# Attention and gated FFN on one core: the RMS scale by a power on GpSimd, the gain at the transposes, scores issued ahead

## The chip, the core and the metric

One NeuronCore of a Trainium2 chip runs the whole program. The metric is the device time of one execution in microseconds. PE is TensorE (matmuls, and transposes as matmuls against an identity), DVE is VectorE, ACT is ScalarE, POOL is GpSimd, and SP only issues DMAs. Each engine works through its own instructions strictly in the order in which the kernel was written, since the whole program stands under a manual schedule; engines wait for each other by semaphores.

## What is computed

Eight batches of causal attention (8 heads, 576 positions, head size 64) whose scores carry a decay, and on its output, read as 4608 tokens of 512, an RMS norm with a gain and a gated FFN:

```
scores = q @ k.T / 8 + min(-(cum_i - cum_j), 0)      # cum: running sum of max(s, 0)
x   = softmax(scores, causal) @ v                    # per batch and head
xn  = x / sqrt(mean(x * x) + 1e-6) * rms_g
out = (silu(xn @ w_gate) * (xn @ w_val)) @ w_out     # 512 -> 1536 -> 512
```

The kernel writes exp(score) as exp(q.k/8) times a weight of the key, which is folded into v (`vw`), so no row maximum is taken. Checks at the end (`check_decay`, `check_all`) set a flag when the inputs don't allow that; a slow general path follows then. It isn't entered here.

## The kernel before

**Stages.** The FFN works in nine chunks of 512 tokens, attention in eight batches of 576. After a start with batch 0 the program alternates between two kinds of stage:

- F(c), c = 0 to 8: the first FFN products of chunk c (`ffn1`). A group (`ffn1_group`, L294) is the gate and value products of one block of 128 hidden units, then Silu on ACT (L302), then the product with the value half on DVE (L303), which frees one of two PSUM buffers `psD`. Chunks 0 to 3 take 256 tokens a group (24 groups), the later ones 512 (12 groups).
- A(b), b = 1 to 7: the attention of batch b, woven with the second FFN product (`ffn2_steps`, 48 matmuls) of chunk b-1. F(8) and its second product end the program.

**Attention.** Eight units of one pair of heads and one half of the queries each. `unit_scores` issues the score matmuls into `psD`, an Exp on ACT and the causal mask on POOL (`affine_select`, L231, for the second half of the units L235 too). `unit_av` (L253 to L258) multiplies with `vw` into one of two `psAV` buffers, and DVE divides by the row sum and writes `x_blk`. Before, AV of unit u stands ahead of the scores of unit u+2.

**RMS norm.** A batch has five blocks of 128 tokens. After unit 4 blocks 0 and 1 are complete: ACT squares and sums them (L265) and `att_alpha` (L268) computes 1/sqrt on DVE by a bit trick and three Newton steps, twelve instructions on 128x2 numbers, and two that scale `x_blk` (L281). Blocks 2 to 4 follow in the next F stage. `att_out` transposes a scaled block on PE (L288, `psX`) and DVE copies it into `xnT` (L292), the FFN's input. The gain `rms_g` is multiplied into the two weight matrices once, on DVE (`scale_w`, L123).

**What stands beside F(c).** Python lists of functions with a position between 0 and 1 (`fillers`): `ffn1` calls each behind the first group whose share of the stage reaches its position. They are the tail of batch c's norm (`tail_fillers`) and the preparation of batch c+1 (`prep_fillers`): repacking of k and q from runs of six positions to one block per transpose (`prep_pack`, L172, on POOL), transposes with their copies, `prep_v` on POOL, and for the check the largest absolute value of every row of KT and QT (`prep_peak`, L191, on DVE). POOL also issues the loads of k and q (which turn fp32 into bf16), and those of v and the weights at the start.

Of the kernel before, what the change touches and what calls it, by code (L numbers as in the profile page):

```python
# [10 lines left out]
def kernel(  # L11
# [108 lines left out]
    def scale_w(which, lo, hi):  # L120
        dst = (wg_sb, wv_sb)[which]
        for cc in range(CC):
            nc.vector.tensor_scalar(  # L123
                out=dst[:, cc, lo:hi], in0=dst[:, cc, lo:hi],
                scalar1=g_sb[:, cc : cc + 1], scalar2=None, op0=ALU.mult)

    def decay_weights():
# [46 lines left out]

    def prep_transpose(b, which, hp):
        src, dst = ((k_nat, KT), (q_nat, QT))[which]
        pT = ps_t()
        for c in range(KC):
            nc.tensor.matmul(pT[:, c, :], lhsT=src[:, c, 2 * hp : 2 * hp + 2, :].rearrange("p h d -> p (h d)"),  # L179
                             rhs=ident_bf[0:KP, 0:KP], is_transpose=True,  # L180
                             start=(c == 0), stop=(c == KC - 1))
        o = dst[:, hp, 0:S].rearrange("p (t c) -> p t c", c=KC)
        i = pT.rearrange("p c t -> p t c")
# [436 lines left out]
```

## Time and profile before

| what | value |
|---|---|
| median of 2 runs | 527.65 us (526.64 to 528.66) |
| the profiled execution's own time | 528.67 us |
| its span, first to last instruction | 527.0 us |
| PE busy | 401.5 us, 76% |
| DVE busy | 313.6 us, 60% |
| ACT busy | 201.4 us, 38% |
| POOL busy | 164.1 us, 31% |
| mean granted clock of PE | 0.902 |

Busy shares are means over the whole span. PEclk is the share of full speed that PE's clock had in a stretch: 1.00 is 2.4 GHz and 0.50 is 1.2 GHz, the only two levels that the records show; a value between is a mixture in time. A row of a timeline gives start and duration of an instruction (or of some equal ones, x4) in us, and in brackets how long its engine had been idle and what released it.

### The profile page before, as it was taken

The numbers are of one execution on the slowest core, as the hardware profiler recorded it, in microseconds if no ns is written. First come the engines' busy times: TensorE is split into PE (matmuls) and PEld (weight loads), VectorE is DVE, ScalarE is ACT, GpSimd is POOL, SyncE is SP. The second block draws the span as 40 slices with busy tenths as digits, with TensorE's granted clock in tenths as the row PEclk, the third lists the DMA queues.
The fourth block names the chain that finished last, engine by engine and source line by source line (L and its number), as shares of the span: only waits on it lengthen the run. The fifth ranks groups of instructions, "written<-read, shape, count | busy, mean of one in ns | idle before, by whom it ended". The sixth has DMA issues, their size and how long they took to land.

```text
span 527.0 us, 8080 instructions
## 1 busy us (share of the span) xinstructions
PE 401.5 (76%) x3092; PEld 240.3 (46%) x3129; DVE 313.6 (60%) x756; ACT 201.4 (38%) x349; POOL 164.1 (31%) x268
## 2 busy tenths in 40 slices
PE   3556589479965899479956898579947997799895
PEld 2334475248633775258533444235422544343442
DVE  5665886746666584747565484747573666433341
ACT  2532236324562247224552247034722465230220
POOL 8565503830067003820076004900381013000000
PEclk9997999779997799689987799689977998899999
DMA  9999541091014701090006601290100001001002
GB/s 144 195 192 207 110 65 41 21 177 25 1 41 80 142 1 41 21 200 2 21 22 109 112 1 41 38 181 1 41 20 21 1 21 42 20 1 60 22 1 85
DMA packets 53069, 33.77 MB, mean 64 GB/s; under 512 B 29856, under 2 KB 47776, under 8 KB 53024
## 3 DMA queue, kind: packets, MB, share of 16 engines
q0 software_dynamic: 19104, 16.52, 20.2%
q1 hardware_dynamic: 33920, 16.67, 13.0%
q8 instruction: 26, 0.43, 0.3%
q14 instruction: 19, 0.16, 0.1%
HBM read 37.90 MB, written 9.44 MB: 90 GB/s over the span
## 4 chain that ended last, share of the span: by engine, by line
PE 58%; DVE 25%; ACT 7%; issue 5%; POOL 2%; DMA 2%; ACTq 0%; POOLq 0%
PE psD L298 29%; PE psO L322 17%; DVE peak L191 4%; ACT sq_scr L265 4%; DVE x_blk L281 4%; DVE H_sb L303 4%; PE psAV L253 3%; PE psD L224 3%; PE psX L288 3%; DVE al L278 3%; DVE al L276 3%; DVE al L277 2%; ACT E L229 2%; PE psT L179 2%; DMA v_nat<-in_v_dram 2%
## 5 line engine op out<-in xcount | busy, mean ns | idle before, releaser
L302 ACT ACTIVATE S_sb<-psD 128x256 bf16<-128x256 f32 (+1 forms) x156 | 72.2, 465 | 272.3 <-PE psD L298 262.6
L298 PE MATMUL psD<-xnT,wg_sb 128*128 128x256 bf16 (+1 forms) x614 | 129.7, 334 | 13.0 <-DVE H_sb L303 10.7
L303 DVE TENSOR_TENSOR H_sb<-S_sb,psD 128x256 bf16<-128x256 bf16 (+1 forms) x156 | 80.5, 520 | 99.2 <-ACT S_sb L302 98.9
L298 PE MATMUL psD<-xnT,wv_sb 128*128 128x256 bf16 (+1 forms) x620 | 126.7, 330 | 0.2
L231 POOL TENSOR_SCALAR_AFFINE_SELECT E<-E 128x512 bf16<-128x512 bf16 x64 | 40.7, 636 | 262.9 <-ACT E L229 262.8
L322 PE MATMUL psO<-wout_sb,H_sb 128*128 128x512 bf16 x409 | 112.2, 409 | 2.9 <-issue 2.7
L298 PEld LDWEIGHTS <-wg_sb 128*128 128x128 bf16 x624 | 61.8, 104 | 48.2 <-issue 20.1
L298 PEld LDWEIGHTS <-wv_sb 128*128 128x128 bf16 x624 | 64.3, 103 | 38.5 <-issue 4.0
L253 PE MATMUL psAV<-vw,E 128*128 128x65 bf16 x576 | 33.4, 207 | 53.8 <-DVE x_blk L258 48.2
L229 ACT ACTIVATE E<-psD 128x1024 bf16<-128x1024 f32 x64 | 64.4, 1021 | 23.9 <-PE psD L224 23.9
L253 PEld LDWEIGHTS <-E 128*128 128x128 bf16 x576 | 28.1, 106 | 72.8 <-DVE x_blk L258 51.7
L322 PEld LDWEIGHTS <-H_sb 128*128 128x128 bf16 x432 | 39.0, 104 | 46.4 <-issue 14.3
L327 DVE COPY osb<-psO 128x512 f32<-128x512 f32 x36 | 24.8, 689 | 44.5 <-PE psO L322 44.5
L288 PE MATMUL psX<-ident_bf,x_blk 128*128 128x128 bf16 x160 | 20.9, 295 | 35.3 <-DVE x_blk L281 34.7
L197 POOL TENSOR_TENSOR vw<-v_nat,wT 128x512 bf16<-128x512 f32 (+1 forms) x35 | 36.5, 1043 | 3.6 <-DMA v_nat<-in_v_dram 3.5
L288 PEld LDWEIGHTS <-x_blk 128*128 128x128 bf16 x160 | 16.5, 137 | 45.3 <-DVE x_blk L281 38.3
L258 DVE TENSOR_TENSOR x_blk<-psAV,rZ 128x256 bf16<-128x256 f32 (+1 forms) x64 | 31.4, 491 | 2.2
L224 PE MATMUL psD<-QT,KT 64*128 64x256 bf16 (+2 forms) x320 | 26.7, 266 | 1.0 <-DVE H_sb L303 1.0
L265 ACT ACTIVATE sq_scr<-x_blk 128x512 bf16<-128x512 bf16 x40 | 25.0, 626 | 0.8
L185 DVE COPY KT<-psT 128x576 bf16<-128x576 bf16 x32 | 24.0, 749 | 1.6 <-PE psT L179 1.5
L172 POOL COPY q_nat<-q_raw 96x768 bf16<-96x768 bf16 x28 | 23.5, 838 | 1.8 <-DMA q_raw<-in_q_dram 1.8
L257 DVE RECIPROCAL rZ<-psAV 128x4 f32<-128x4 f32 (+1 forms) x64 | 11.7, 183 | 20.7 <-PE psAV L253 20.7
(72 smaller groups left out, 350.2 us busy)
## 6 DMA issues: line engine op xcount, KB each, us to landing
out_dram<-osb SPq DMA_DIRECT2D x36, 256.0 KB, 2.0
v_nat<-in_v_dram SPq DMA_DIRECT2D x24, 256.0 KB, 8.0
k_raw<-in_k_dram POOLq DMA_DIRECT2D x7, 576.0 KB, 6.4
q_raw<-in_q_dram POOLq DMA_DIRECT2D x7, 576.0 KB, 10.0
v_nat<-in_v_dram POOLq DMA_DIRECT2D x8, 256.0 KB, 14.3
wg_sb<-in_moe_w_gate_dram POOLq DMA_DIRECT2D x4, 384.0 KB, 14.0
wv_sb<-in_moe_w_val_dram POOLq DMA_DIRECT2D x4, 384.0 KB, 15.6
wout_sb<-in_moe_w_out_dram POOLq DMA_DIRECT2D x2, 768.0 KB, 19.1
```

Of the source, the lines that this page charges most:

```text
L197: eng.tensor_tensor(out=vw[0:n, sc, :, 0:64], in0=v_nat[0:n, b % 2, sc, :, :], in1=wb.unsqueeze(2).to_broadcast([n, H, D]), op=ALU.mult)
L224: nc.tensor.matmul(st[:, j, c0 : c0 + q1 - q0], lhsT=KT[rs, hp, kb * 128 : kb * 128 + 128], rhs=QT[rs, hp, q0:q1], start=(i == 0), stop=(i ...
L229: nc.scalar.activation(out=E, in_=st, func=AF.Exp, scale=0.125)
L231: nc.gpsimd.affine_select(out=diag, in_=diag, pattern=[[0, 4], [1, 128]], compare_op=ALU.is_ge, fill=0.0, base=0, channel_multiplier=-1)
L253: nc.tensor.matmul(AV[:, j, qb - q0, :], lhsT=E[:, j, c0 : c0 + 128], rhs=vw[:, kb, h, :], start=(j == 0 and i == 0), stop=(j == 1 and i = ...
L258: nc.vector.tensor_tensor(out=a.x[:, q0 : q0 + nq, hp * 128 : (hp + 1) * 128].rearrange("p t (j d) -> p j t d", j=2), in0=AV[:, :, :, 0:64 ...
L265: nc.scalar.activation(out=sq_scr, in_=a.x[:, tb, :], func=AF.Square, accum_out=a.ss[:, tb : tb + 1])
L288: nc.tensor.matmul(X[:, cc, :], lhsT=a.x[:, tb, cc * 128 : (cc + 1) * 128], rhs=ident_bf, is_transpose=True, start=(cc == 0), stop=(cc == ...
L298: nc.tensor.matmul(P[:, j, 0:n], lhsT=w[:, cc, fb * 128 : (fb + 1) * 128], rhs=xnT[:, cc, t0 + o : t0 + o + n], start=(cc == 0), stop=(cc ...
L302: nc.scalar.activation(out=sl[:, 0:n], in_=P[:, 0, 0:n], func=AF.Silu)
L303: nc.vector.tensor_tensor(out=Ht[:, fb, o : o + n], in0=sl[:, 0:n], in1=P[:, 1, 0:n], op=ALU.mult)
L322: nc.tensor.matmul(O, lhsT=Ht[:, fb, tb * 128 : (tb + 1) * 128], rhs=wout_sb[:, fb, :], start=(fb == 0), stop=(fb == FB - 1))
```

## The change

- `att_alpha` is two GpSimd instructions: mean plus epsilon, and that to the power -0.5. The scaling of a block is a function of its own, `att_scale`, on DVE: for blocks 0 and 1 it stands two units later than the squares (behind unit 6), for blocks 2 to 4 right ahead of each block's transpose.
- `rms_g` is multiplied in where `xnT` is written; `scale_w` is gone.
- k and q of batches 2 to 7 are loaded in blocks of 128 positions (ten DMAs a batch, each run 64 numbers long, into double buffers) and need no repacking; batches 0 and 1 are still repacked, on DVE, with the free end of `xnT` as buffers. The loads of batch c+2 stand at 0.1 of F(c).
- The scores of unit u+2 stand ahead of AV of unit u, and the second FFN product is dealt out 8, 4, 6 matmuls around the first scores.
- The check keeps the largest absolute value of QT only, in the A stage; for k it takes sums of squares on ACT (`prep_norm`).
- A group of chunks 0 to 3 holds two hidden blocks, so that Silu and product work on 512 columns; the weights come in two pieces each instead of four.

```diff
     def att_alpha(a, t0, t1):
...
+        nc.gpsimd.tensor_scalar(out=m, in0=a.ss[:, t0:t1], scalar1=1.0 / DM, scalar2=1e-6,
                                 op0=ALU.mult, op1=ALU.add)
-        nc.vector.tensor_scalar(out=y.bitcast(i32), in0=m.bitcast(i32), scalar1=-0.5,
-                                scalar2=1597463007.0, op0=ALU.mult, op1=ALU.add)
...
+        nc.gpsimd.tensor_tensor(out=y, in0=m, in1=mhalf[:, 0 : t1 - t0], op=ALU.pow)
+
+    def att_scale(a, tb):
+        nc.vector.tensor_scalar(out=a.x[:, tb, :], in0=a.x[:, tb, :],
+                                scalar1=a.al[:, 1, tb : tb + 1], scalar2=None, op0=ALU.mult)
...
-        nc.vector.tensor_copy(out=xnT[:, :, c0 : c0 + 128 - p0], in_=X[:, :, p0:128])
+        nc.vector.tensor_tensor(
+            out=xnT[:, :, c0 : c0 + 128 - p0], in0=X[:, :, p0:128],
+            in1=g_sb.unsqueeze(2).to_broadcast([128, CC, 128 - p0]), op=ALU.mult)
...
     def tail_fillers(a, lo, hi):
-        fns = [lambda: [att_square(a, tb) for tb in (2, 3, 4)], lambda: att_alpha(a, 2, 5)]
-        fns += [lambda tb=tb: att_out(a, tb) for tb in (2, 3, 4)]
+        fns = [lambda tb=tb: att_square(a, tb) for tb in (2, 3, 4)]
+        fns += [lambda: att_alpha(a, 2, 5)]
+        fns += [lambda tb=tb: (att_scale(a, tb), att_out(a, tb)) for tb in (2, 3, 4)]
         return spread(fns, lo, hi)
...
         for u in range(2 * HP):
-            unit_av(a, u)
             if u + 2 < 2 * HP:
                 unit_scores(a, u + 2)
+            unit_av(a, u)
             if u == HP:
-                att_square(a, 0)
-                att_square(a, 1)
+                for tb in (0, 1):
+                    att_square(a, tb)
                 att_alpha(a, 0, 2)
+            if u == HP + 2:
+                for tb in (0, 1):
+                    att_scale(a, tb)
...
             if c + 2 < B:
-                fillers.append((0.65 if c else 0.96, lambda b=c + 2: (load_kq(b, 0), load_kq(b, 1),
-                                                       load_v(b, nc.sync))))
+                for w in range(2):
+                    fillers.append((0.1, lambda b=c + 2, w=w: load_kq(b, w)))
+                fillers.append((0.1, lambda b=c + 2: load_v(b, nc.sync)))
```

The order on GpSimd (POOL) behind the attention of batch 0, before: loads of k and q (L98), of `wout` (L111) and of v (L105) for batch 1, and then the repacking.

```order
L235 AFFINE_SELECT E<-E 128x2x64
L98 DMA k_raw<-in_k_dram 96x8x384
L98 DMA q_raw<-in_q_dram 96x8x384
L111 DMA wout_sb<-in_moe_w_out_dram 128x6x512 x2
L105 DMA v_nat<-in_v_dram 128x8x64 x4
L105 DMA v_nat<-in_v_dram 64x8x64
L172 COPY k_nat<-k_raw 96x6x128
```

The same place now; `xnT` stands for the borrowed buffers of k and q, L105 loads k and q of batch 2, L318 and L320 are the scale of blocks 2 to 4 of batch 0.

```order
L111 DMA xnT<-in_k_dram 96x8x384
L111 DMA xnT<-in_q_dram 96x8x384
L124 DMA wout_sb<-in_moe_w_out_dram 128x6x512 x2
L118 DMA v_nat<-in_v_dram 128x8x64 x4
L118 DMA v_nat<-in_v_dram 64x8x64
L105 DMA k_nat<-in_k_dram 128x8x64 x4
L105 DMA k_nat<-in_k_dram 64x8x64
L105 DMA q_nat<-in_q_dram 128x8x64 x4
L105 DMA q_nat<-in_q_dram 64x8x64
L318 TENSOR_SCALAR al<-ss 128x3
L320 TENSOR_TENSOR al<-al,mhalf 128x3
```

Ten more DMA issues stand ahead of the scale on POOL; in F(1) to F(5) the same ten stand ahead of it, without the nine rows of batch 1 and `wout`.

The order on VectorE (DVE) late in A(1), before: the end of the twelve-step scale and the scaling of blocks 0 and 1, and behind them the reciprocals and products (L257, L258) that free the `psAV` buffers.

```order
L277 TENSOR_TENSOR al<-al 128x2
L278 SCALAR_TENSOR_TENSOR al<-al 128x2
L281 TENSOR_SCALAR x_blk<-x_blk,al 128x512 x2
L257 RECIPROCAL rZ<-psAV 128x6
L258 TENSOR_TENSOR x_blk<-psAV,rZ 128x2x3x64
L257 RECIPROCAL rZ<-psAV 128x6
L258 TENSOR_TENSOR x_blk<-psAV,rZ 128x2x3x64
```

The same place now, with L305 and L306 for these two lines, L378 for the copy of a finished output block, and L323 for the scaling.

```order
L305 RECIPROCAL rZ<-psAV 128x6
L306 TENSOR_TENSOR x_blk<-psAV,rZ 128x2x3x64
L378 COPY osb<-psO 128x512
L305 RECIPROCAL rZ<-psAV 128x6
L306 TENSOR_TENSOR x_blk<-psAV,rZ 128x2x3x64
L323 TENSOR_SCALAR x_blk<-x_blk,al 128x512 x2
L305 RECIPROCAL rZ<-psAV 128x6
L306 TENSOR_TENSOR x_blk<-psAV,rZ 128x2x3x64
```

Three of the last units were freed behind the scale; now only the last one is, and behind the scaling alone.

The order on VectorE (DVE) at the start of F(1), before: products of the first two groups, the scale of three blocks, then products and copies into `xnT` in turn.

```order
L278 SCALAR_TENSOR_TENSOR al<-al 128x3
L281 TENSOR_SCALAR x_blk<-x_blk,al 128x512 x3
L303 TENSOR_TENSOR H_sb<-S_sb,psD 128x256
L292 COPY xnT<-psX 128x4x128
L303 TENSOR_TENSOR H_sb<-S_sb,psD 128x256 x2
L292 COPY xnT<-psX 128x4x128
L303 TENSOR_TENSOR H_sb<-S_sb,psD 128x256
L292 COPY xnT<-psX 128x4x64
```

The same place now: L352 is the product of a group, L323 the scaling of one block, L334 the write into `xnT`.

```order
L352 TENSOR_TENSOR H_sb<-S_sb,psD 128x2x256 x3
L323 TENSOR_SCALAR x_blk<-x_blk,al 128x512
L334 TENSOR_TENSOR xnT<-psX,g_sb 128x4x128
L352 TENSOR_TENSOR H_sb<-S_sb,psD 128x2x256
L323 TENSOR_SCALAR x_blk<-x_blk,al 128x512
L334 TENSOR_TENSOR xnT<-psX,g_sb 128x4x128
L352 TENSOR_TENSOR H_sb<-S_sb,psD 128x2x256
L323 TENSOR_SCALAR x_blk<-x_blk,al 128x512
L334 TENSOR_TENSOR xnT<-psX,g_sb 128x4x64
```

The three scalings stood together, ahead of a product; now each stands behind the product of the group just issued.

## Rows read from the trace of the kernel before

**Rows 1.** Seven A stages by windows: stretch, its length, busy time per engine, PEclk, DMA, GB/s.

```profile
81.40:107.33 25.93, 18.08 (x166) 9.67 (x169) 16.71 (x39) 12.25 (x15) 17.31 (x29) 0.87 0.09 32
...
427.29:448.97 21.68, 17.69 (x166) 9.70 (x169) 12.91 (x39) 12.46 (x15) 6.07 (x12) 0.92 0.10 37
sum 180.57, PE 128.57 PEld 68.78 DVE 109.85 ACT 86.41 POOL 112.83; mean PE 18.37 PEld 9.83 DVE 15.69 ACT 12.34 POOL 16.12
```

**Rows 2.** Seven F stages, F(1) to F(7), by windows.

```profile
165.78:198.51 32.73, 27.52 (x253) 22.83 (x252) 20.94 (x54) 12.83 (x33) 2.70 (x5) 0.90 0.49 82
...
sum 213.88, PE 182.98 PEld 117.12 DVE 128.72 ACT 79.17 POOL 9.24; mean PE 26.14 PEld 16.73 DVE 18.39 ACT 11.31 POOL 1.32
```

**Rows 3.** F(8), which has nothing beside it, by windows.

```profile
489.44:510.18 20.74, 20.64 (x97) 9.41 (x98) 7.70 (x12) 6.57 (x11) 0.00 (x0) 1.00 0.00 1
```

**Rows 4.** Waits of PE's attention and transposes on VectorE: total us, times, longest.

```profile
PE psAV L253 <- DVE x_blk L258: 48.2, 7, 7.5
...
PE psX L288 <- DVE x_blk L281: 34.7, 9, 4.6
```

**Rows 5.** Timeline of A(2): start, duration, engine, line, operation; in brackets idle time and releaser.

```profile
153.53 0.16 DVE L276 TENSOR_TENSOR al<-al 128x2 f32<-128x2 f32 x1
...
154.90 0.82 POOL L172 COPY k_nat<-k_raw 96x768 bf16<-96x768 bf16 x1
...
155.77 0.73 DVE L276 TENSOR_TENSOR al<-al 128x2 f32<-128x2 f32 x1
...
158.08 2.47 DVE L281 TENSOR_SCALAR x_blk<-x_blk,al 128x512 bf16<-128x512 bf16 x2
...
161.29 0.84 PE L253 MATMUL psAV<-vw,E 128*128 128x65 bf16 x12 [7.48 <-DVE x_blk L258]
```

**Rows 6.** Timeline of A(7).

```profile
440.22 1.00 ACT L229 ACTIVATE E<-psD 128x1024 bf16<-128x1024 f32 x1
...
441.29 0.64 POOL L231 TENSOR_SCALAR_AFFINE_SELECT E<-E 128x512 bf16<-128x512 bf16 x1 [1.39 <-ACT E L229]
...
444.36 0.84 PE L253 MATMUL psAV<-vw,E 128*128 128x65 bf16 x12 [3.33 <-DVE x_blk L258]
```

**Rows 7.** Timeline of F(5), its first groups.

```profile
343.64 0.60 ACT L302 ACTIVATE S_sb<-psD 128x512 bf16<-128x512 f32 x1 [13.93 <-PE psD L298]
...
344.27 0.69 DVE L303 TENSOR_TENSOR H_sb<-S_sb,psD 128x512 bf16<-128x512 bf16 x1 [1.67 <-ACT S_sb L302]
...
348.56 0.88 DVE L281 TENSOR_SCALAR x_blk<-x_blk,al 128x512 bf16<-128x512 bf16 x3
348.97 0.61 PE L288 MATMUL psX<-ident_bf,x_blk 128*128 128x128 bf16 x4 [3.65 <-DVE x_blk L281]
```

**Rows 8.** The stretch behind F(2)'s first wait, by windows.

```profile
170.87:177.70 6.83, 5.12 (x29) 3.88 (x30) 3.67 (x15) 0.77 (x2) 0.00 (x0) 0.50 1.25 233
```

**Rows 9.** Groups by line and form: busy us, mean ns of one, idle before.

```profile
L197 POOL TENSOR_TENSOR vw<-v_nat,wT 128x512 bf16<-128x512 f32 x28 | 29.2, 1042 | 3.6 <-DMA v_nat<-in_v_dram 3.5
...
L292 DVE COPY xnT<-psX 128x512 bf16<-128x512 bf16 x32 | 13.4, 421 | 5.0 <-PE psX L288 5.0
...
L200 POOL COPY vw<-wT 128x8 bf16<-128x8 bf16 x28 | 6.1, 218 | 0.0
```

**Rows 10.** Timeline of GpSimd from 34 to 56 us.

```profile
34.73 1.81 POOL L105 DMA_DIRECT2D v_nat<-in_v_dram  x2
...
39.41 0.88 POOL L105 DMA_DIRECT2D v_nat<-in_v_dram  x1 [1.30 <-DMA wv_sb<-in_moe_w_val_dram]
43.56 0.70 POOL L105 DMA_DIRECT2D v_nat<-in_v_dram  x1 [3.27 <-DMA k_raw<-in_k_dram]
...
55.88 1.04 POOL L197 TENSOR_TENSOR vw<-v_nat,wT 128x512 bf16<-128x512 f32 x1 [3.52 <-DMA v_nat<-in_v_dram]
```

**Rows 11.** The page's table of DMA issues: KB of each, median us from issue to landing.

```profile
v_nat<-in_v_dram SPq DMA_DIRECT2D x24, 256.0 KB, 8.0
...
v_nat<-in_v_dram POOLq DMA_DIRECT2D x8, 256.0 KB, 14.3
```

More of the change, by code (lines that the diff above doesn't have):

```diff
@@ L45 @@
     CUM_MAX = 150.0
-    DOT_MAX = 12.0
+    QK_MAX = 200.0
     pers = ctx.enter_context(tc.tile_pool(name="pers", bufs=1))
@@ L93, in ps_t, with load_kq, load_runs @@
     def ps_t():
-        return pp.tile([128, KC, KP], bf16, name="psT", tag="AT", bufs=2)
-    def load_kq(b, which, h0=0, h1=H):
+        return pp.tile([128, NB * 128], bf16, name="psT", tag="AT", bufs=2)
+    def load_kq(b, which):
+        dst, src = ((k_nat, k), (q_nat, q))[which]
+        for sc in range(NB):
+            n = 128 if sc < 4 else 64
+            nc.gpsimd.dma_start(
+                out=dst[0:n, b % 2, sc, :, :],
+                in_=src[b, :, sc * 128 : sc * 128 + n, :].rearrange("h p d -> p h d"))
+    def load_runs(b, which, h0=0, h1=H):
         dst, src = ((k_raw, k), (q_raw, q))[which]
@@ L118, in load_w, with decay_a @@
                 in_=src[:, lo:hi].rearrange("(cc p) f -> p cc f", p=128))
[L120 to L127, printed above, removed]
+    def decay_a():
         nc.vector.tensor_scalar(out=s_all, in0=s_all, scalar1=0.0, scalar2=None, op0=ALU.max)
@@ L175, in prep_transpose @@
     def prep_transpose(b, which, hp):
-        src, dst = ((k_nat, KT), (q_nat, QT))[which]
+        dst = (KT, QT)[which]
         pT = ps_t()
[L178 to L183, printed above, removed]
+        if b < 2:
+            src = (k_pk, q_pk)[which]
+            t = pT[:, 0:S].rearrange("p (c t) -> p c t", c=KC)
+            for c in range(KC):
+                nc.tensor.matmul(t[:, c, :],
+                                 lhsT=src[:, c, 2 * hp : 2 * hp + 2, :].rearrange("p h d -> p (h d)"),
+                                 rhs=ident_bf[0:KP, 0:KP], is_transpose=True,
+                                 start=(c == 0), stop=(c == KC - 1))
+            o = dst[:, hp, 0:S].rearrange("p (t c) -> p t c", c=KC)
+            i = t.rearrange("p c t -> p t c")
+        else:
+            src = (k_nat, q_nat)[which]
+            for sc in range(NB):
+                n = 128 if sc < 4 else 64
+                nc.tensor.matmul(
+                    pT[:, sc * 128 : sc * 128 + n],
+                    lhsT=src[0:n, b % 2, sc, 2 * hp : 2 * hp + 2, :].rearrange("p h d -> p (h d)"),
+                    rhs=ident_bf[0:n, 0:n], is_transpose=True,
+                    start=(sc == 0), stop=(sc == NB - 1))
+            o, i = dst[:, hp, 0:S], pT[:, 0:S]
@@ L306, in ffn1 @@
     def ffn1(c, plan, fillers):
         Ht = mp.tile([128, FB, DM], bf16, name="H_sb", tag="H_sb", bufs=2)
-        done, total = 0, len(fillers)
-        for i, (o, n, fb) in enumerate(plan):
-            ffn1_group(Ht, c * DM, o, n, fb)
-            while done < total and fillers[done][0] <= (i + 1) / len(plan):
+        fillers = sorted(fillers, key=lambda f: f[0])
+        done = 0
+        for i, (o, n, f0) in enumerate(plan):
+            ffn1_group(Ht, c * DM, o, n, f0)
+            while done < len(fillers) and fillers[done][0] <= (i + 1) / len(plan):
@@ L312, in ffn1 @@
                 fillers[done][1]()
                 done += 1
-        assert done == total
+        assert done == len(fillers)
         return Ht
```

237 lines of the change are left out of this document (131 added, 106 removed).

## The prediction

> **What bounds the kernel now.** I read the windows by stage first, then the list of waits, then the timelines. No engine is busy throughout; the end is set by PE, which works or waits for one particular thing. The seven A stages take 180.57 us in sum, 25.8 each, of which PE is busy 18.4 [rows 1]; the seven F stages take 213.88 us, 30.6 each [rows 2]. F(8), with nothing beside it, is PE at full clock for 20.74 us, or 1.73 for each of 12 groups [rows 3]. Two waits fill most of the difference, one in each kind of stage: AV on `x_blk`, seven times, 48.2 us, and the transposes `psX` on the scaled block, nine times, 34.7 us [rows 4].
>
> The first is DVE's order. In A(2) the twelve steps of the scale stand on DVE ahead of the products that free `psAV`. A step takes 0.16 us alone, but 0.73 as soon as POOL's repacking runs beside it, whose copies take 0.82, and the two scalings take 2.47 [rows 5] where three take 0.88 alone [rows 7]. So PE waits 7.48 us for AV of unit 6 [rows 5]. A(7) has no repacking beside it, since there is no batch 8, and shows what is left without it: a wait of 3.33 and 21.68 us in all [rows 1, 6]. The second is 3.65 us at the start of F(5) [rows 7]. Behind such a wait the granted clock falls: after F(2)'s it was 0.50, that is 1.2 GHz, for 6.83 us in which PE was busy 5.12 [rows 8], so about half of that, 2.6 us, is lost.
>
> **The change part by part.** *A stages.* Scale and repacking leave DVE's order and POOL's neighbourhood, and the scaling stands behind the freeing of unit 6. Take A(7): 21.68 less the wait of 3.33 is 18.35. Its PEclk of 0.92 says that 16% of it, 3.5 us, ran at the lower level [rows 1]; without the wait the clock has no reason to fall, so half of that, 1.7, goes too. What is late next: Exp of unit 7 still stands behind the two squares on ACT, and takes 1.00, its mask 0.64 and a smaller one behind it [rows 6]. PE reaches AV of unit 7 about 1.0 us before that, since scores now come earlier and nothing else holds it. Writing `xnT` with the gain is a product from PSUM instead of a copy: between 0.42, the copy [rows 9], and 0.69, the product of that size [rows 7]; I take 0.69, and 0.3 of it shows at the stage's end. That makes 18.35 - 1.7 + 1.0 + 0.3 = 17.95, say 18.0 for each of seven, 126.0 instead of 180.57: **-54.6**. The peaks of QT that move here are DVE work, hidden since DVE was busy 12.91 of 21.68 in A(7) with the scale in it [rows 1].
>
> The two GpSimd instructions that replace the scale are not in the trace. The nearest rows are a copy of 128x8, 0.22, and a product of 128x512, 1.04 [rows 9]; I take 0.25 each, for 2 or 3 numbers per partition. The next thing on POOL is the mask of unit 7, due about 1.0 us after the squares, so 0.5 is hidden; at 1.04 each, 1.1 us of each A and up to 1.6 of each F would show.
>
> *F stages, c = 1 to 7.* The old wait of 3.65 goes, but another takes its place, three times. A block's scaling now stands on DVE behind the product of the group just issued, and PE's next instruction is that block's transpose. So PE waits for Silu 0.60, product 0.69 and 0.41 from the scaling's start to the transpose: 1.70 for each of three blocks, 5.1 [rows 7]. POOL starts the five `prep_v` (1.04 each [rows 9]) right behind the scale, and scaling suffers from such neighbours as rows 5 show: 2.47 for two is about 0.9 more each; I take 0.5 for two of the three, 1.0. Net +5.1 + 1.0 - 3.65 = +2.45 for c = 1 to 6, and +1.45 for c = 7, which prepares nothing: **+16.2**. In F(1) to F(5) ten DMA issues (0.9 each, from 1.81 for two [rows 10]) stand on POOL ahead of the scale. They need no data, so they start at the mask of unit 7, some 3 us before F(c) begins (AV of the last unit, its product, two blocks' transposes and six FFN matmuls lie between), and end about 6 us into it, just when the third square does; late by 0 to 1, which I put at 0. The clock I let fall as often as before, since the waits are shorter but three: 0, with bounds in the rivals. Double groups (fewer waits for a Silu) and squares for k on ACT I set against each other at 0.
>
> *F(0).* Here the ten issues do cost. POOL waits with a DMA until its eighth predecessor has landed: the fourth v load waited 1.30 for the last weights, the eighth before it, and the fifth 3.27 for k [rows 10]. Now the scale of batch 0's tail stands behind ten more issues, the last of which needs the second k piece to have landed, which itself queues behind `wout` and v of batch 1. The first v piece landed at 55.88 [rows 10]; four more and two new ones at some 2 us, the last issue 0.70 and the scale make 59 us (56 to 63). PE, which has two groups done by then, waits. From there: ten groups of 1.73, eleven sets of transposes at 0.25 (0.61 at the lower clock [rows 7]), two waits of 1.70, and about 4 for a PE that starts at 1.2 GHz (2.6 above, for a longer stretch): 59 + 17.3 + 2.8 + 3.4 + 4 = 86.5, against 81.4 now [rows 1]: **+5**. That A(0) ends earlier, with fewer weight DMAs ahead of its masks and no `scale_w`, is swallowed by this wait.
>
> *The rest* (the end of the program, the longer check) I put at 0; it is a few small instructions between F(7) and F(8).
>
> Sum, against the profiled execution: span 527.0 - 54.6 + 16.2 + 5 = 493.6, and 1.67 around it (528.67 - 527.0) gives 495.3. That execution lies 1.0 above the median of 527.65, so on the median's scale **494**. About 2% (10.6 us) is what a measurement of this kernel can tell from no change.
>
> Two pages speak against parts of this. Rows: v in pieces of 256 bytes from SP lands 8.0 us after issue [rows 11]. The Trainium skill, DMA: Bandwidth & Descriptors, section Specifications, wants transfers of at least 512 bytes for line rate, and k and q now go to 128-byte pieces. By that rule the loads would land late, which is the third rival below; by the row they don't matter a period ahead. And the Trainium skill, TensorE: Matmul & The Clock Gate, section "A second HAM failure mode", tells of a PE that pauses between groups of matmuls and goes back and forth between its clocks. By that every F would run partly at 1.2 GHz, the second rival; no row before shows three short pauses in a row.
>
> **The rivals.** *1. The clock holds in F.* Waits of 1.7 leave PE busy half of the time; the falls in the rows stand behind waits of 3.3 and more [rows 6 to 8]. Then 2.6 comes back in six stages: 494 - 16 = 478. *2. It stays low through all three waits of F.* Then some three groups run at half speed, 1.73 each, 5 more in F(1) to F(6): 494 + 30 = 524. *3. Slower: POOL's ten issues hold the scale back in every F.* If a piece lands 14.3 us after issue, the median of POOL's v loads in the crowded start [rows 11], instead of the few that I assume, the tenth issue waits for the second piece until 12 us into F, and the scale comes some 7 late in F(1) to F(5): 494 + 36 = 530. It decides from 6.7 us late in each, where the 33.5 are used up; at 20 us to land it is 557. For it: rows 10, where POOL did wait so. Against: outside the start the queues are all but empty in A [rows 1], 0.09 of the engines' time. *4. The wait only moves to POOL.* If the power is slow, the mask of unit 7 is late, and A(b) keeps A(7)'s 3.33: 28 of the 54.6 are not gained: 522.
>
> **How the numbers follow.** Forecast 0.52, first rival 0.25, second 0.09, third 0.06, fourth 0.08. Faster by over 2% (under 517) are the forecast, the first rival and a part of the second and fourth: 0.87; within 2%: 0.09; slower: 0.04. The range is 472 to 515: below, rival 1 with F(0) at 56 instead of 59 and a short POOL pair; above, F(0) at 63 (+4), A stages of 19 (+7) and half of rival 2 (+10).
>
> **What would show it.** Right: PE's wait for AV of unit 6 is gone from the list of waits and A stages are 17 to 19 us; `psX` waits for the scaling three times per F, 1.7 to 2.5 each; in F(0) PE stands from some 32 to 59 us while POOL issues L105. Wrong: a long POOL row for L320, PE waiting for masks in A, or F(1) to F(5) much longer than F(6).

## The result, and the profile after

| | before | after |
|---|---|---|
| median | 527.65 us | 506.08 us (505.74 to 506.42, 2 runs) |
| span of the profiled execution | 527.0 us | 504.7 us |
| PE, DVE, ACT, POOL busy | 401.5, 313.6, 201.4, 164.1 us | 395.9, 230.7, 215.1, 172.3 us |
| mean granted clock of PE | 0.902 | 0.925 |

The ratio is 0.9591, 95% interval 0.9508 to 0.9675: faster, by 21.6 us where 33.6 were forecast (494, range 472 to 515). The lengths by stage, from the first matmul of each to that of the next, show where the forecast was off:

| term, us | predicted | measured |
|---|---|---|
| A(1) to A(7) | -54.6 | -55.6 (sum 124.9, each 17.85) |
| F(1) to F(7) | +16.2 | +12.1 (sum 226.0) |
| end of F(0) | +5 | +18.2 (99.6 instead of 81.4) |
| chunk 7's second product, the check, F(8) and the last product | 0 | +3.1 (54.2 instead of 51.1) |
| span | 493.6 | 504.7 |

The changed kernel by windows: A(2), F(2), the wait in F(0), the rest of F(0), F(8). Columns as in [rows 1].

```profile
150.89:168.74 17.85, 17.05 (x170) 8.02 (x168) 12.09 (x28) 12.35 (x15) 9.86 (x18) 1.00 0.24 53
168.74:202.13 33.39, 27.41 (x245) 22.58 (x244) 13.21 (x22) 13.35 (x27) 12.02 (x16) 0.95 0.73 76
32.00:64.78 32.78, 0.38 (x5) 0.11 (x2) 1.82 (x2) 1.83 (x5) 12.27 (x16) 0.57 1.71 187
64.78:99.60 34.82, 25.98 (x220) 20.75 (x221) 16.34 (x30) 13.59 (x25) 4.14 (x6) 0.82 0.05 4
464.47:487.99 23.52, 23.52 (x98) 10.08 (x97) 8.31 (x16) 6.57 (x11) 0.00 (x0) 0.88 0.00 1
```

In A, PE is now busy 17.05 of 17.85 at full clock [rows 1: 25.93 at 0.87]. F and F(0) are not so full. The list of waits answers to [rows 4].

```profile
PE psX L330 <- DVE x_blk L323: 77.5, 25, 32.4
...
PE psT L201 <- DVE xnT L191: 7.8, 7, 1.7
...
PE psAV L301 <- POOL E L279: 4.3, 8, 0.6
```

The 48.2 us of AV on `x_blk` are gone; 4.3 on masks are left, 0.6 at the last unit of each A. The wait for scaled blocks has grown from 9 times to 25, three in each F, the longest 32.4 in F(0). New is a wait of batch 1's transposes on DVE's repacking. The tail of F(2), from its timeline, answers to [rows 7].

```profile
173.16 0.69 DVE L352 TENSOR_TENSOR H_sb<-S_sb,psD 128x512 bf16<-128x512 bf16 x1 [1.16 <-ACT S_sb L351]
...
174.67 0.89 POOL L320 TENSOR_TENSOR al<-al,mhalf 128x3 f32<-128x3 f32 x1
...
175.53 5.07 POOL L237 TENSOR_TENSOR vw<-v_nat,wT 128x512 bf16<-128x512 f32 x5
175.59 1.13 DVE L323 TENSOR_SCALAR x_blk<-x_blk,al 128x512 bf16<-128x512 bf16 x1
...
176.78 0.61 PE L330 MATMUL psX<-ident_bf,x_blk 128*128 128x128 bf16 x4 [2.63 <-DVE x_blk L323]
...
177.18 1.91 PE L345 MATMUL psD<-xnT,wg_sb 128*128 128x256 bf16 x8
...
181.75 0.35 DVE L323 TENSOR_SCALAR x_blk<-x_blk,al 128x512 bf16<-128x512 bf16 x1
...
182.16 0.40 PE L330 MATMUL psX<-ident_bf,x_blk 128*128 128x128 bf16 x4 [1.67 <-DVE x_blk L323]
...
185.97 0.40 PE L330 MATMUL psX<-ident_bf,x_blk 128*128 128x128 bf16 x4 [1.68 <-DVE x_blk L323]
```

The pow on three numbers per partition takes 0.89. The first scaling, beside POOL's products of v, takes 1.13, the second, after them, 0.35. PE waits 2.63, 1.67 and 1.68, 5.98 in all, and the eight matmuls behind the first wait take 1.91 instead of 1.04. F(0), on POOL and then on PE (a timeline of each):

```profile
43.93 0.89 POOL L105 DMA_DIRECT2D k_nat<-in_k_dram  x1 [3.86 <-DMA xnT<-in_q_dram]
48.55 0.88 POOL L105 DMA_DIRECT2D k_nat<-in_k_dram  x1 [3.73 <-DMA wout_sb<-in_moe_w_out_dram]
...
54.63 0.87 POOL L105 DMA_DIRECT2D k_nat<-in_k_dram  x1 [0.37 <-DMA v_nat<-in_v_dram]
...
59.88 2.43 POOL L105 DMA_DIRECT2D q_nat<-in_q_dram  x3 [0.36 <-DMA v_nat<-in_v_dram]
62.39 0.20 POOL L318 TENSOR_SCALAR al<-ss 128x3 f32<-128x3 f32 x1
62.67 0.88 POOL L320 TENSOR_TENSOR al<-al,mhalf 128x3 f32<-128x3 f32 x1
```

```profile
64.78 0.61 PE L330 MATMUL psX<-ident_bf,x_blk 128*128 128x128 bf16 x4 [32.40 <-DVE x_blk L323]
65.18 1.91 PE L345 MATMUL psD<-xnT,wg_sb 128*128 128x256 bf16 x8
...
77.64 1.04 PE L345 MATMUL psD<-xnT,wv_sb 128*128 128x256 bf16 x8
...
85.59 0.43 PE L201 MATMUL psT<-ident_bf,xnT 96*128 96x96 bf16 x6 [1.68 <-DVE xnT L191]
...
89.51 0.43 PE L201 MATMUL psT<-ident_bf,xnT 96*128 96x96 bf16 x6 [1.48 <-DVE xnT L191]
```

POOL stands with its issues until transfers have landed, so the scale of batch 0's tail, whose squares ACT had done by 33.4, comes at 62.39.

### The profile page after: what moved, and what is told of

Its sections match the earlier page's. It is cut to its first block, busy times and chain, and to the rows that moved or that the text cites. A ratio compares the mean times of both kernels' runs of the same rounds, so it can differ in the third digit from the quotient of the medians.

```text
span 504.7 us, 7722 instructions
## 1 busy us (share of the span) xinstructions
PE 395.9 (78%) x3083; PEld 226.9 (45%) x3083; DVE 230.7 (46%) x461; ACT 215.1 (43%) x351; POOL 172.3 (34%) x267
## 3 DMA queue, kind: packets, MB, share of 16 engines
q0 software_dynamic: 63840, 16.52, 34.5%
## 4 chain that ended last, share of the span: by engine, by line
PE 57%; DMA 12%; POOL 10%; DVE 9%; ACT 8%; issue 4%; SPq 0%; ACTq 0%; POOLq 0%
PE psD L345 35%; PE psO L373 11%; DMA v_nat<-in_v_dram 8%; PE psT L211 4%; PE psX L330 3%; DMA xnT<-in_k_dram 3%; DVE H_sb L352 3%; ACT S_sb L351 3%; DVE x_blk L323 2%; POOL al L320 2%; POOL q_nat L105 2%; PE psAV L301 2%; ACT E L277 2%; POOL E L279 2%; PE psD L272 2%
## 5 line engine op out<-in xcount | busy, mean ns | idle before, releaser
L351 ACT ACTIVATE S_sb<-psD 128x512 bf16<-128x512 f32 x108 | 64.3, 595 | 240.1 <-PE psD L345 239.7
L352 DVE TENSOR_TENSOR H_sb<-S_sb,psD 128x512 bf16<-128x512 bf16 x108 | 74.2, 687 | 165.1 <-ACT S_sb L351 165.1
L345 PE MATMUL psD<-xnT,wg_sb 128*128 128x256 bf16 (+1 forms) x624 | 121.9, 335 | 0.0
L345 PE MATMUL psD<-xnT,wv_sb 128*128 128x256 bf16 (+1 forms) x624 | 118.3, 327 | 0.0
L279 POOL TENSOR_SCALAR_AFFINE_SELECT E<-E 128x512 bf16<-128x512 bf16 x64 | 41.1, 642 | 213.1 <-ACT E L277 212.9
L373 PE MATMUL psO<-wout_sb,H_sb 128*128 128x512 bf16 x432 | 107.4, 379 | 0.0
L330 PEld LDWEIGHTS <-x_blk 128*128 128x128 bf16 x160 | 10.6, 104 | 90.6 <-DVE x_blk L323 87.6
L378 DVE COPY osb<-psO 128x512 f32<-128x512 f32 x36 | 24.8, 688 | 29.1 <-PE psO L373 29.1
L237 POOL TENSOR_TENSOR vw<-v_nat,wT 128x512 bf16<-128x512 f32 (+1 forms) x35 | 35.5, 1044 | 0.0
L323 DVE TENSOR_SCALAR x_blk<-x_blk,al 128x512 bf16<-128x512 bf16 x40 | 18.9, 489 | 29.8 <-POOL al L320 29.3
L306 DVE TENSOR_TENSOR x_blk<-psAV,rZ 128x256 bf16<-128x256 f32 (+1 forms) x64 | 31.4, 491 | 2.2
L334 DVE TENSOR_TENSOR xnT<-psX,g_sb 128x512 bf16<-128x512 bf16 (+1 forms) x40 | 24.8, 636 | 14.3 <-PE psX L330 13.7
L105 POOL DMA_DIRECT2D k_nat<-in_k_dram x30 | 25.8, 880 | 12.2 <-DMA wout_sb<-in_moe_w_out_dram 7.7
L105 POOL DMA_DIRECT2D q_nat<-in_q_dram x30 | 25.4, 901 | 1.6 <-DMA v_nat<-in_v_dram 1.6
```

The source lines that it names most:

```text
L105: nc.gpsimd.dma_start(out=dst[0:n, b % 2, sc, :, :], in_=src[b, :, sc * 128 : sc * 128 + n, :].rearrange("h p d -> p h d"))
L237: eng.tensor_tensor(out=vw[0:n, sc, :, 0:64], in0=v_nat[0:n, b % 2, sc, :, :], in1=wb.unsqueeze(2).to_broadcast([n, H, D]), op=ALU.mult)
L279: nc.gpsimd.affine_select(out=diag, in_=diag, pattern=[[0, 4], [1, 128]], compare_op=ALU.is_ge, fill=0.0, base=0, channel_multiplier=-1)
L306: nc.vector.tensor_tensor(out=a.x[:, q0 : q0 + nq, hp * 128 : (hp + 1) * 128].rearrange("p t (j d) -> p j t d", j=2), in0=AV[:, :, :, 0:64 ...
L330: nc.tensor.matmul(X[:, cc, :], lhsT=a.x[:, tb, cc * 128 : (cc + 1) * 128], rhs=ident_bf, is_transpose=True, start=(cc == 0), stop=(cc == ...
L345: nc.tensor.matmul(P[:, j, i * n : (i + 1) * n], lhsT=w[:, cc, fb * 128 : (fb + 1) * 128], rhs=xnT[:, cc, t0 + o : t0 + o + n], start=(i = ...
```

## The experiments

**1. F(0): the place of POOL's issues.** `load_kq` of batch 2 alone moves behind batch 0's tail.

```diff
-fillers.append((0.1, lambda b=c + 2, w=w: load_kq(b, w)))
+fillers.append((0.1 if c else 0.3, lambda b=c + 2, w=w: load_kq(b, w)))
```

> Edit: in F(0) alone the ten k/q loads of batch 2 (and the v loads behind them) are issued behind batch 0's tail instead of ahead of its scale; everything else is the changed kernel. Theory (it is POOL's wait for its own transfers that holds PE until 64.78): the scale runs right behind the last v issue, which ended at 40.1, so PE resumes at 41 to 44 instead of 64.8 and F(0) ends at 76 to 81 instead of 99.6; the later stages keep their lengths; 506 - 20 = 486 us (482 to 491). Rival (F(0) waits for the crowded queues themselves: batch 1's k and q, wout, v land no earlier): PE resumes early but stands again at batch 1's transposes, and F(0) ends at 90 or later: 496 or more.

Measured 487.4 us (ratio to before 0.9201, 0.9154 to 0.9249). F(0) ends at 79.13, 20.5 earlier, and the scale stands at

```profile
40.90 0.69 POOL L118 DMA_DIRECT2D v_nat<-in_v_dram  x1 [3.29 <-DMA xnT<-in_k_dram]
41.66 0.20 POOL L318 TENSOR_SCALAR al<-ss 128x3 f32<-128x3 f32 x1
```

so PE resumes at 43.27. The theory holds: with this place alone moved back, F(0) ends 2 us earlier than before the change, not 18 later. F(1) was 36.6 instead of 33.4, at the same three waits but a clock of 0.81 (see the last section).

**2. F(0): the repacking of batch 1.** `prep_pack` goes one group ahead of its transposes.

```diff
-for h in range(0, H, 2) for w in range(2)], lo - 0.06, hi - 0.06)
+for h in range(0, H, 2) for w in range(2)], lo - 0.14, hi - 0.14)
```

> Edit: the changed kernel with batch 1's eight repacking copies in F(0) issued one FFN1 group earlier, nothing else. Read by stage: F(0) ends at 99.6 in the changed kernel. Theory (four times in F(0) PE waits 1.5 to 1.7 because the repacking stands on DVE behind the product of the group just issued, and the transposes directly behind it): the four waits go and F(0) ends at 93 to 95. Rival (the copies of KT on DVE and QT on ACT, which free the two psT buffers, are as late as the packs): the waits move there and F(0) ends at 97 or later.

F(0) took 66.68 instead of 71.94, and from PE's resumption to its end 29.1 instead of 34.8. Of the 7.8 us of waits on L191 the list has 2.1 left, none of them in F(0); two waits of 0.29 on the copies of KT are what the rival has. The end was at 94.83, within the theory's range. The one run took 497.78 us, 8.3 less than the changed kernel: 4.8 is F(0)'s earlier end, 2.8 is F(8), which this edit doesn't touch (see 6).

**3. F(c): the transposes one group behind the scaling.**

```diff
-fns += [lambda tb=tb: (att_scale(a, tb), att_out(a, tb)) for tb in (2, 3, 4)]
...
+(0.23, lambda: att_scale(a, 2)),
+(0.30, lambda: (att_out(a, 2), att_scale(a, 3))),
+(0.38, lambda: (att_out(a, 3), att_scale(a, 4))),
+(0.46, lambda: att_out(a, 4))]
```

> Edit: in F(1) to F(7) each scaling of a tail block is issued one FFN1 group ahead of that block's transposes, instead of directly before them. Theory (PE waits three times per F because the scaling stands behind the product of the group just issued, 0.60 + 0.69 + 0.4 us): a whole group of 1.73 now covers each of the three, so the waits of 2.6, 1.7 and 1.7 go, and with them the stretch at clock 0.5 behind the first; F(1) to F(6) 26 to 28 instead of 33.3, F(7) 20 to 22 instead of 26.9; 506 - 43 = 463 us (456 to 472). Rival (what is late is the scale itself, behind squares on ACT and ten issues on POOL): the first wait stays at 2 or more and the clock falls behind it as now; only the other two go, 3.4 per F: 482 us.

Measured 459.06 us (0.8683, 0.8648 to 0.8718): one order of instructions is worth more than the whole change was. F(1) to F(7) sum to 180.1 instead of 226.0; PE's waits in them fall from 40.5 to 5.2, and the clock is 1.00 in all seven. F(2) by windows:

```profile
161.61:188.13 26.52, 25.64 (x246) 21.86 (x244) 13.40 (x22) 13.47 (x27) 12.07 (x16) 1.00 0.92 96
```

One wait of 0.88 is left in F(2), behind the scaling that POOL's products slow.

**4. F(c): POOL's ten issues in F(1) to F(5).** They go behind the scale, F(0) stays.

```diff
+fillers.append((0.45 if c else 0.1, lambda b=c + 2, w=w: load_kq(b, w)))
```

> Edit: the changed kernel with POOL's ten k/q issues (and SP's v issues) of F(1) to F(5) behind the tail's scale instead of ahead of it; F(0) as in the changed kernel. Read by stage: F(1) to F(5) 33.2 to 33.4 against F(6), which has no issues, 32.4. Theory (the ten issues end 0.6 us after the last square, so they hold the scale back by that much and no more): F(1) to F(5) 32.3 to 32.7, in all about 4 us less: 502. Rival (they hold the scale back by several us): F(1) to F(5) 30 or less. Rival 2 (issues now beside the scalings slow these as POOL's products do): 33.5 or more.

506.15 us in one run, no gain, and F(1) to F(5) took 32.1, 33.9, 38.2, 31.5 and 33.2: none of the three expectations fits. The first wait did shrink, from 2.63 to 2.03, as the theory said. In F(3) the third grew from 1.68 to 2.58: two of POOL's products now stand behind the issues and beside the third scaling, which took 1.25. But in sum the waits stayed at 5.4 to 6.3, so the spread of the lengths comes from elsewhere. F(3) and F(4) by windows, and their waits:

```profile
219.00:257.23 38.23, 31.89 (x246) 24.85 (x246) 13.66 (x22) 13.47 (x28) 15.01 (x19) 0.78 0.68 70
274.89:306.34 31.45, 25.45 (x147) 12.36 (x149) 13.15 (x22) 13.34 (x27) 14.89 (x19) 1.00 0.82 84
```

```profile
226.44 0.40 PE L330 MATMUL psX<-ident_bf,x_blk 128*128 128x128 bf16 x4 [2.03 <-DVE x_blk L323]
...
231.45 0.61 PE L330 MATMUL psX<-ident_bf,x_blk 128*128 128x128 bf16 x4 [1.68 <-DVE x_blk L323]
...
238.04 0.61 PE L330 MATMUL psX<-ident_bf,x_blk 128*128 128x128 bf16 x4 [2.58 <-DVE x_blk L323]
...
282.31 0.40 PE L330 MATMUL psX<-ident_bf,x_blk 128*128 128x128 bf16 x4 [2.07 <-DVE x_blk L323]
...
286.13 0.40 PE L330 MATMUL psX<-ident_bf,x_blk 128*128 128x128 bf16 x4 [1.70 <-DVE x_blk L323]
...
290.32 0.40 PE L330 MATMUL psX<-ident_bf,x_blk 128*128 128x128 bf16 x4 [2.07 <-DVE x_blk L323]
```

F(3) waits 6.29 us in three pieces, F(4) 5.84, and they differ by 6.8 us: the one ran partly at 1.2 GHz (0.78), the other at 2.4 throughout. That F(3) takes 256 tokens a group and F(4) 512 doesn't explain it; in the changed kernel they take 33.4 and 33.2.

**5. A(b): the scale back on DVE.** Four runs take A apart. First `att_alpha` with its twelve steps on `nc.vector`, nothing else:

```diff
-nc.gpsimd.tensor_tensor(out=y, in0=m, in1=mhalf[:, 0 : t1 - t0], op=ALU.pow)
...
+for _ in range(3):
+    nc.vector.tensor_tensor(out=t, in0=y, in1=y, op=ALU.mult)
...
```

> Edit: the two GpSimd instructions of the scale are put back as the twelve small DVE steps of the kernel before; scaling, loads and orders stay as in the changed kernel. Theory (pow on GpSimd itself gains little; the late scaling and the missing repacking are what shortened A, and POOL's queue is what lengthened F(0)): twelve steps of 0.16 us on DVE lengthen A by 1 to 2 each (+10) and F by 0.5 to 1 each (+5), and F(0), whose scale no longer stands behind POOL's ten issues, ends some 20 earlier: 506 + 15 - 20 = 501 us (494 to 508). Rival 1 (the steps on DVE are what made the long wait of A): A goes back to 21.7, as A(7) was: 506 + 27 + 5 - 20 = 518. Rival 2 (F(0)'s length is not the scale's place on POOL): F(0) still ends near 99, total 515 to 525.

533.89 us (1.0106, 1.0057 to 1.0155): the whole gain is lost; against the kernel before it is 1% longer, within the 2% that count as the same. My theory of the pow fell. Its first rival is right for A (22.2 instead of 17.85, 21.7 expected), but its total of 518 is not, since F(1) to F(7) take 2.6 more each. F(0) ends at 81.3, as all but the second rival had it. A(2) of this run:

```profile
152.34 0.17 DVE L318 TENSOR_SCALAR al<-ss 128x2 f32<-128x2 f32 x1 [0.98 <-ACT sq_scr L313]
...
153.29 0.64 POOL L279 TENSOR_SCALAR_AFFINE_SELECT E<-E 128x512 bf16<-128x512 bf16 x1 [1.39 <-ACT E L277]
153.34 0.60 DVE L324 TENSOR_TENSOR al<-al 128x2 f32<-128x2 f32 x1
...
154.88 0.19 DVE L305 RECIPROCAL rZ<-psAV 128x6 f32<-128x6 f32 x1
...
155.72 0.84 PE L301 MATMUL psAV<-vw,E 128*128 128x65 bf16 x12 [2.32 <-DVE x_blk L306]
156.37 1.47 PE L380 MATMUL psO<-wout_sb,H_sb 128*128 128x512 bf16 x3
```

The steps hold unit 5's product back behind 154.88, AV of unit 7 waits 2.32 for the `psAV` buffer that it frees, and the three matmuls behind take 1.47, where they took 0.81 at full clock. In all of A(2) PE's waits are 2.2 more than in the changed kernel, and its busy time is 2.4 more (19.44 for 17.05, clock 0.86 for 1.00): wait and clock make half of the 4.4 us each.

Then the two scalings also back to their old place, and on top of that eight POOL copies a batch of the old repacking's shape (from the weights into a scratch tile, feeding nothing):

```diff
                 att_alpha(a, 0, 2)
+                for tb in (0, 1):
+                    att_scale(a, tb)
```

> Edit: as the run with the twelve steps back on DVE, and the two scalings of an attention stage also go back to their old place directly behind the steps, ahead of the products of units 5 to 7. Read by stage, A(1) to A(7) (17.85 in the changed kernel, 22.2 with the steps alone, 25.8 before). Theory (in A, PE's wait is the sum of what stands on DVE ahead of the product that frees a psAV buffer): the scalings put some 0.7 us more ahead of unit 5's product, so the wait of 2.3 becomes 3.0 and A 22.5 to 23.5. Rival (once the steps are there, the place of the scalings makes no difference, because AV of unit 7 waits for its mask anyway): 22.0 to 22.4. F(c) as with the steps alone; about 535 us in all.

> Edit: as the run before in this call, and POOL gets eight copies of 96x768 in each of F(1) to F(6), directly behind the masks, of the shape of the old repacking (they copy weights into a scratch tile and feed nothing). Read by stage, A(1) to A(6) against A(7), whose F(7) has no copies. Theory (POOL's copies slow DVE's steps and scalings beside them, as in the old kernel): A(1) to A(6) 24 to 26, A(7) stays at 22 to 23. Rival (copies behind the last mask come too late to touch the steps; the rest of the old length came from scores standing behind AV): A(1) to A(6) within 0.5 of A(7). Total about 550 by the theory, 540 by the rival.

532.07 and 567.38 us, one run each. The place of the scalings adds 0.2 (A(1) to A(5) 22.4), which looks like its rival; but the wait in A(2) is

```profile
155.02 0.54 PE L301 MATMUL psAV<-vw,E 128*128 128x65 bf16 x12 [3.41 <-DVE x_blk L306]
```

so it grew by 1.1, even more than the theory's 0.7, and a clock of 0.92 instead of 0.86 hid it. The copies add 1.2 (23.5 to 23.8), short of the theory's 24, with a wait of 5.12 in A(2) at a clock of 0.93. In F(1) to F(5) they add 5.6 (41.1 against 35.5): with POOL's ten issues behind them they push the products of v beside the steps of the next scale, the first of which takes 4.03 in F(2). F(6) has the copies and no issues, and took 34.5 against 35.3. A(7) was 20.6 in both runs, without the copies too, at a clock of 1.00; so it is no measure for A(1) to A(6), as the expectation took it. Last, AV ahead of the scores as before:

```diff
+            unit_av(a, u)
             if u + 2 < 2 * HP:
                 unit_scores(a, u + 2)
-            unit_av(a, u)
```

> Edit: the changed kernel with AV of a unit issued ahead of the scores two units on, as before the change, and nothing else. Read by stage, A(1) to A(7) (17.85 in the changed kernel). Theory (scores ahead of AV bring Exp and mask of unit 7 forward by one AV, 0.4 to 0.5 us, which matters only at the last unit): 18.3 to 18.8, about 510 us in all. Rival 1 (the order carries much of the gain of A): 20 or more, over 520. Rival 2 (it carries nothing): 17.8 to 18.0.

A 18.84: the order of the scores is worth 1.0, more than my 0.4 to 0.9 and far from Rival 1; here the clock was 1.00 in both, and 0.8 of it is the wait for the mask. Yet the total of the one run was 502.42, below the changed kernel: F(1) to F(7) sum to 219.2 instead of 226.0, and F(8) took 20.73. F(2) by windows was

```profile
167.98:200.02 32.04, 25.84 (x245) 21.74 (x244) 13.43 (x22) 13.34 (x27) 12.08 (x16) 1.00 0.76 79
```

with waits of 2.63, 1.90 and 1.68, 0.2 more than the changed kernel's, and yet 1.35 us shorter, at a clock of 1.00 instead of 0.95.

**6. The end: the check in four pieces.** `check_all` is cut and issued between groups of F(8).

```diff
+        return [(0.05, check_decay), (0.2, s0), (0.4, s1), (0.6, s2)]
...
-                check_decay()
-                check_all()
+                fillers += check_steps()
```

> Edit: the check of norms and decay, which stood in one piece between FFN2(7) and FFN1(8), is cut into four pieces that are issued between groups of F(8). Theory (the chain of small DVE and PE steps makes PE stand 3.44 us and the clock fall behind it): the gap before F(8) goes (-3.4) and F(8) runs at full clock, 20.8 instead of 23.5 (-2.7), for 0.3 to 0.6 of short PE steps in between: 506 - 5.6 = 500.5 us (499 to 502). Rival (the fall of the clock has to do with the start of F(8) whatever precedes it): only the gap goes, 502.5 to 503.5. Rival 2: each piece makes PE wait for DVE in F(8): no gain.

500.08 us (0.9453, 0.9411 to 0.9495). The stretch from the start of chunk 7's second product to the end of F(8) is 31.8 instead of 37.5, -5.7 as forecast: the gap of 3.4 is gone and F(8) is 21.42 at a clock of 1.00. Only the gap is shown to be the check's doing. With the check in one piece and the same waits (1.95, 0.47 and 0.24) F(8) ran at 0.88 to 0.94 in the changed kernel and the runs of 1, 3 and 4, but at 1.00, in 20.73, in that of 2 and all four of 5. F(8) of 2, and that of this run:

```profile
458.44:479.17 20.73, 20.62 (x97) 9.42 (x97) 8.30 (x16) 6.57 (x11) 0.00 (x0) 1.00 0.00 1
...
460.18:481.60 21.42, 21.42 (x103) 9.56 (x102) 10.30 (x26) 6.57 (x11) 0.00 (x0) 1.00 0.04 13
```

So the four pieces cost F(8) 0.7 against those runs, and the 2.1 that it gained against the changed kernel is clock that also came back without them.

**7. All of it together.** Experiments 2, 3 and 6; POOL's issues and products of v in the second half of F; F(0) in halves, so that six groups stand ahead of batch 0's tail; the squares of batch 0's k a little earlier.

> Edit: the changed kernel with all that the runs so far point to: transposes one group behind their scalings (as measured: F 26.5 instead of 33.4), the check spread over F(8) (-5.7), the ten k/q issues and the v products of POOL in the second half of each F, F(0) in halves so that six groups instead of three stand ahead of batch 0's tail, and batch 1's repacking one group ahead of its transposes. Theory: F(0) starts at 28.3 and needs 12 x 1.75 + 4.5 of transposes + some 6 of waits for weights and scale + 2 of clock: ends at 60 to 66 instead of 99.4; F(1) to F(6) lose the rest wait of 0.9 as scalings no longer run beside POOL's products: 25.5; total 457 - 36 - 5.7 - 5 = 412 us (404 to 424). Rival (the transfers of the start bound F(0): v of batch 1 lands at 56 to 60 whatever the order): A(1) waits for vw, and the total is 425 to 435.

> Edit: the combined kernel of the call before, with the ten k/q issues of F(0) ahead of the products of v instead of behind them, so that POOL spends the time in which it waits for v of batch 1 on issuing. Theory (in the combined kernel the masks of A(1) wait for POOL, which issues until 69.8, and AV of unit 0 waits 3.1): POOL's issues, which wait for landings, end at 62 and the products at 67.5, so AV waits 0 to 1, A(1) is 17.9 to 19 instead of 20.9, F(0) stays: 417 us (415 to 419). Rival (the issues ahead hold the products back as much as they gain): no change, 419 to 421.

419.46 us (0.7936, 0.7919 to 0.7954) and 417.50 us (0.7905, 0.7891 to 0.7920): both kernels are beaten, the changed one by 17%. In the first F(0) ended at 62.28 as expected, but A(1) took 20.87, since POOL issued until 69.8 and the masks stood behind. In the second it is 21.66 and F(0) ends 1.8 earlier:

```profile
62.20 5.05 POOL L246 TENSOR_TENSOR vw<-v_nat,wT 128x512 bf16<-128x512 f32 x5
...
67.48 1.81 POOL L288 TENSOR_SCALAR_AFFINE_SELECT E<-E 128x512 bf16<-128x512 bf16 x3
```

The total came as forecast, but not by the way forecast: AV still waits 2.43 for the mask, now behind the products. That is 0.7 less than in the first (3.13), yet A(1) is 0.8 longer, at a clock of 0.92 instead of 1.00.

## Why the prediction was right, and where not

**A stages, right to 1 us.** The wait went and, as the prediction had it, the clock didn't fall: measured 17.85 for 17.95 to 18.0, at 1.00. Inside the sum two small errors cancel: the wait for unit 7's mask is 0.60 where 1.0 stood, and PE's work 17.05 where 21.68 - 3.33 - 1.7 = 16.65 stood. One reading was wrong, without effect on the sum: the AV that waited 7.48 [rows 5] is not unit 6's. It is the last of A(2)'s four AVs of twelve matmuls, those of units 4 to 7, so unit 7's, and the buffer it waited for is freed by unit 5's product. What the prediction gave as one sum experiment 5 splits. In the lengths, the twelve steps put back on DVE are 4.4 of the 8.0 us that an A lost, the place of the scalings on top of them 0.2, the copies on top of both 1.2, and the order of the scores, put back alone, 1.0. These lengths hold different clocks, so the waits are the better measure: PE's waits in A(2) grew by 2.2, 0.9, 1.4 and 0.8, and in the first three runs it came to its long wait at the same time, 14.1 us into the stage. They were 7.96 in all before and 0.60 after, so about 2 us of wait are not assigned; that the parts add up was not tried.

**F stages, the three waits right, the clock and the double groups mis-sized.** Three waits were forecast at 5.1 + 1.0 and measured 5.98; experiment 3 shows that they are what they were said to be, the scaling behind the group's product. Two terms that were put at 0 were not. The clock did not fall "as often as before": F(1) to F(7) had been at 0.89 to 0.95, which makes 37.5 us at 1.2 GHz, and were at 0.95 six times and at 1.00 in F(7), which makes 20.5 us. By [rows 8], 2.6 lost of 6.83, the difference of 17 is worth some 6 us, an estimate. And of the groups of 256 tokens, F(1) to F(3) lost waits of 1.3 a stage for `psD`, which are gone now that a group is double. So +12.1 near +16.2 is in part luck: the stages with +2.45 in the forecast grew by +0.5, +0.7, +1.5 in F(1) to F(3) and +2.8, +4.4, +2.2 in F(4) to F(6), and F(7), whose waits came as forecast (5.03), by +0.05 for +1.45. The ten issues cost the scale 0.6 in F(1) to F(5), inside the 0 to 1 given.

**F(0), the mis-sized term: +5, measured +18.2.** That POOL's ten issues hold the scale back was right (experiment 1: their place alone moves F(0)'s end by 20.5). Two numbers in it failed. PE's resumption, put at 59, came at 64.78. The first piece of v did not come late: it had landed by 54.63, where 55.88 was taken. But the seven issues from there took 7.7, four of them 1.2 to 1.5 each, behind one landing after the other, and the last three 2.4, where 2.7 stood; the scale took 1.2 where two times 0.25 stood; and another 1.2 went to the first scaling, 1.13 beside POOL's products, which had no term. And the 27.5 from there took 34.8: the four waits of the repacking on DVE, 6.1 in sum, are not in the prediction at all, and most of the rest is the clock, at 0.50 to 77.64: PE was busy 10.1 us of that, half of which is 5.1, where 4 stood. It saw that a scaling right ahead of its transpose makes PE wait for Silu and product, and didn't see that the same holds for packs ahead of transposes. Experiment 2 makes F(0) 5.3 shorter.

**The end, put at 0, cost 3.1.** "A few small instructions" are a chain over DVE and PE in which each waits for the other. Its gap is 0.4 longer than before's, and that is all that the longer check is shown to cost. F(8), at 1.00 before [rows 3], ran at 0.88 behind it, 2.8 longer; but five runs with the same check had it at 1.00 (experiment 6), so the 2.8 is the clock, whose fall there is not explained.

**The rivals.** The clock (first and second) came out between the two: F(1) to F(6) all ran partly at 1.2 GHz, but only for 3.4 us each (0.95). In experiments 2, 4 and 5 single F stages with the same three waits ran at 1.00, so the first rival's condition does occur. The third, scale late by 7 in every F, did not happen: the pieces of k and q landed soon, as the page's table of DMA issues has them.

```profile
k_nat<-in_k_dram POOLq DMA_DIRECT2D x24, 128.0 KB, 4.5
q_nat<-in_q_dram POOLq DMA_DIRECT2D x24, 128.0 KB, 7.9
```

The Trainium skill, DMA: Bandwidth & Descriptors, section Specifications, asks for transfers of 512 bytes and more for line rate; by that rule these loads, in shorter pieces, run below it. The trace doesn't show their rate against longer ones; it shows that they had landed 4.5 and 7.9 us after issue and were needed a whole period later. The fourth rival's wait was 0.6 per A instead of 3.3. The pow's price, bounded by 0.25 and 1.04, is 0.70 to 0.89, nearer the upper row, plus 0.2 for the mean; the margin ahead of the mask hid most of it.

## What to carry to other kernels

A function that is dealt out between groups should not be followed at once by its own consumer on the engine that must not stop: put producer and consumer one group apart; here that was worth 47 us, some 35 of them waits and the rest mostly clock. On an engine that also issues DMAs, an issue is a possible wait for an older transfer, so nothing urgent stands behind it in the crowded part of the program. Ask of a chain of tiny instructions not what it costs but what is queued behind it.
